# Attention and SoLU MoE on one core: the first two heads' products with v change from float32 to float16 parts, and the planner gets another transfer model

## The chip, the cores and the metric

The kernel runs on one core of a Trainium2 chip. Its time is the device time in microseconds (us) of that core, from launch to end; below it "span" is the part of it from the first to the last instruction of the profile. Engines are named as in the profile: PE is TensorE's matmul side and PEld its weight load, DVE VectorE, ACT ScalarE, POOL GpSimd, SP SyncE, which issues all DMA transfers here.

## The reference

Attention over 4 batches of 8 heads, 1152 keys of 64 dimensions, with queries averaged in pairs to 576 rows, and then a gated block over the 2304 resulting tokens of 512:

```python
q_pool = q.reshape(B, H, S // factor, factor, D).mean(axis=3)
scores = scale * np.matmul(q_pool, k.transpose(0, 1, 3, 2))
attn = softmax(scores)                       # max, exp, sum
x = np.matmul(attn, v)                       # (4, 8, 576, 64) -> (2304, 512)
...
h = x @ w_in
e = np.exp(h - h_max)
solu = h * e / (np.sum(e) + 1e-09)
ln = (solu - mu) / np.sqrt(var + 1e-06) * g_ln
return ln @ w_out
```

## The kernel before

**Tiles and stages.** The 32 heads are numbered 0 to 31, in 16 pairs P that share their loads. A head has 9 slots: in a slot, 128 keys against all 576 queries. A slot's scores are four float32 matmuls of 288 columns (`product`, rows `bank<-q,w`: high and low parts of q and k, in two halves f). ScalarE takes their exponentials, and TensorE multiplies these with v (`values`), adding over the 9 slots of a head in one PSUM bank. The products are made accurate by parts: in slots that are not "whole", ScalarE computes each exponential twice, once into a float16 tile `eh` and once into a float32 tile `e` (called e32 in the code), GpSimd subtracts (`rest`, row `eh<-e,eh`) so that the second half of the tile `eh` holds the float16 remainder, and `values` runs 15 float16 matmuls (`bank<-vhi,eh` and `bank<-vlo,eh`) for a slot in heads 0 to 7, 14 later. v itself is split per pair into `vhi` and `vlo` with a scale (`v_sum`, `v_turn`, `v_mul`, `v_hi`, `v_lo`). In "whole" slots, those below `KP["F"]`, here 18 and so heads 0 and 1, one exponential goes into a float32 tile `eh` and `values` runs 5 float32 matmuls with v as it is loaded (`vx`); the trace shows each as two instructions. These two heads need no `rest` and no split of v.

**Before a head's scores** come its maxima: 12 or 15 float32 matmuls of 384 columns (`bank<-w,q`), each followed by a DVE maximum (`mx<-bank`). Before these come, for each pair: loads of q, k and v; TensorE transposes; high and low parts of k and q by ACT and DVE; and copies from one half of the partitions to the other, by DMA (`k_put`: `w<-khi`, `w<-klo`; `k_again`: `w<-w`; `q_beside`: `q<-q`; the rows of maxima, `put`: `q<-c`).

**Weights** w_in and w_out come in 16 parts of 512 KB (`weight_part`, rows `raw<-in_moe_w_in_dram` and `..._w_out_dram`), each unpacked by two ACT passes (`up`, `un`), one POOL pass (`up<-up,un`), DVE and ACT passes, during heads 0 to 7. The gated block on finished tokens (`tokens`) is interleaved from head 8 on, and its last part runs alone behind head 31.

**What sets the order.** `Plan` collects all operations with a due time `at` in slots, simulates the five engines with a length for each operation, and writes the instructions out in the order of the simulated starts. An engine then executes its queue strictly in this order. A transfer's end in the simulation is: issue time plus a start delay, behind the transfers before it, plus its length `DMA(n)`, plus a delay for landing. The numbers of `KP` are due times and paces: `W` and `step` of the weight parts, `M` of the gated block, `P` of a pair's loads and splits, `N` of the maxima's lead, `CD` which slots take the float16 exponential by a DVE cast (`eh<-e`, L995) instead of a second ACT pass, `VM` who scales v, `F` the number of whole slots. TensorE gets filler transposes of the identity (`bank<-ident`) while it would wait at the start.

Of the kernel before, what the change touches and what calls it, by code (L numbers as in the profile page):

```python
# [17 lines left out]
ALU = mybir.AluOpType  # L18
AXX = mybir.AxisListType.X

KP = {'W': [2, 4, 5], 'step': 0.5, 'M': [77, 15.3, 7.49], 'TX': 113, 'TP': 72, 'win': 5.01, 'P': [22.92, 18.98, 13.92, 23.51, 26.08, 30.44], 'N': [13, 7], 'AV': 3.97, 'CD': [73, 13], 'VM': 'BCCCCABCBABBCCAC', 'AH': 8, 'OF': [5.14, 2.07, 10.29, 1.04, 2.66], 'N1': 10.46, 'warm': 1, 'ws': 1.3, 'GR': 1, 'GG': 12, 'b_eh': 6, 'b_w1': 4, 'V0': -53.76, 'VF': 1, 'QD': [0, 1], 'L0': 0.97, 'F': 18}
FIRST = KP.get("L0", 0.3)


# [15 lines left out]
class Plan:  # L40
# [61 lines left out]
    def run(self):  # L102
# [82 lines left out]
        while events:  # L185
# [67 lines left out]
                kind = o.kind  # L253
                length *= 1 if t > self.COLD else 2
            if e == "SP":
                busy[e] = t + 670 * o.calls
                dma = max(dma, t + 1100) + length
                o.end = dma + 1000
            else:
                busy[e] = o.end = t + length  # L260
            if o.mark is not None:
# [32 lines left out]
    return 1.885 * n + 148  # L294


def DMA(n, fast=1):
    return n / (360 if fast else 180)


@with_exitstack
def attention_solu_moe(
# [157 lines left out]
    def weight_part(n, at, src, i, f, dst_h, dst_l, dst):  # L460
# [15 lines left out]
            else:  # L476
                nc.sync.dma_start(out=raw, in_=src[rows, c])

        add("SP", DMA(4096 * 128), at - 3, fetch, [], [("raw", n)])
        if wide:  # L480


# [59 lines left out]
    def pair(P, at_k, at_q, at_v, loads):  # L542
# [23 lines left out]
        def load_v32(i):  # L566
            nc.sync.dma_start(out=v32(P)[:, i, :, 0:D], in_=v[b, h0 + i].rearrange("(p j) d -> p j d", j=NJ))
# [7 lines left out]
        kb = 128 * NJ * D * 4  # L575
        KT = ("vx", 0, "kt") if P == FN == 1 else ("kt", P)
        if P:
            add("SP", DMA(2 * kb, 0), at_lk, load_k, [("vx", 0, 0, "one")] if P == FN == 1 else [], [KT], calls=2)
        else:
            add("SP", DMA(kb), at_lk, lambda: load_k0(0), [], [("kt", 0, 0)])  # L580
        add("SP", DMA(2 * kb), at_lq, load_q, [], [("qt", P, i) for i in range(3)])
        if not P:
            add("SP", DMA(kb), at_lk + 0.1, lambda: load_k0(1), [], [("kt", 0, 1)])
        if P < FN:
            for i in range(2):
                add("SP", DMA(kb, 0), at_lv + i / 10, lambda i=i: load_v32(i), [], [("vx", 0, P % 2, "v", i)])
# [149 lines left out]
        def prep_q2(at):  # L736
            for i in range(2):
                ps, a = ("qps", (P, i)), at + 2 * i
                add("PE", TR(3 - i), a, lambda i=i: q_tr2(i), [("qt", P, 0)], [ps], also=[("q1", P), ("q2", P)], kind="whole")
                for odd in range(2):  # L740
                    n, o = ((384, 384), (256, 128))[i][odd], a + odd / 10
                    hi, lo = ("q1", P, i, odd), ("q2", P, 2 * i + odd)
                    add("ACT", ACT(n), o, lambda i=i, odd=odd: q_hi2(i, odd), [ps], [hi])
                    add("DVE", DVE(n), o, lambda i=i, odd=odd: q_lo2(i, odd), [ps, hi], [lo])
            for odd in range(2):
                add("SP", DMA(64 * 4 * 576, 0), at + 3, lambda odd=odd: q_beside(odd),
                    [("q1", P, i, odd) for i in range(2)], [("q1", P, 2, odd)], calls=2)
# [205 lines left out]
    def scores(g, at):  # L953
# [452 lines left out]
```

## Time and profile before

| | us |
|---|---|
| median of 3 runs | 729.42 (728.45 to 732.87) |
| the profiled execution | 732.07 |
| its span | 730.3 |
| PE busy | 686.0 (94%) |
| ACT busy | 534.7 (73%) |
| DVE busy | 506.5 (69%) |
| POOL busy | 486.4 (67%) |

Shares over the whole span mix stages. The stages here are the start (up to the first scores at 23.66 us), heads 0 and 1 (to 61.85), heads 2 to 7 (to 171.20), heads 8 to 30 (to 637.06), and head 31 with the rest of the gated block. Matmuls are pipelined, so a row's mean length is longer than the step from one matmul to the next; for matmuls the step is what loads TensorE.

### The profile page before, as it was taken

The page shows a single profiled execution, that of the slowest core. Times are in us where ns is not written, and L with a number is a line of the kernel's source. Part 1 is how long each engine was busy: PE and PEld are TensorE (multiplying, and loading weights), DVE is VectorE, ACT ScalarE, POOL GpSimd, SP SyncE. Part 2 cuts the span into 40 slices and gives each one's busy share as a digit, 9 for nine tenths or more (in the row PEclk, how much of TensorE's full clock was granted, in tenths as well). Part 3 has the DMA queues.
Part 4 walks back from the last instruction along what each step waited for, and adds up shares of the span by engine and source line. Part 5 has one row for each costly group of instructions (what it writes and reads, how often), then busy time and mean ns, then how long its engine had stood idle before and what let it go on. Part 6 is the DMA issues. An engine that isn't in the chain of part 4 may idle for free.

```text
span 730.3 us, 18791 instructions
## 1 busy us (share of the span) xinstructions
PE 686.0 (94%) x7048; PEld 598.7 (82%) x7048; DVE 506.5 (69%) x1221; ACT 534.7 (73%) x1327; POOL 486.4 (67%) x635
## 2 busy tenths in 40 slices
PE   7999787999989999999998999899999999999996
PEld 7989676777877888887887898788888898887885
DVE  5896786787887677877858684858586867425542
ACT  2656797989797687888778796778788877773432
POOL 1233796989788678697868677686967777681111
PEclk8999898999999999999999999999999999999999
DMA  8585566674453352536253434425445310000011
GB/s 206 156 210 152 152 161 160 180 182 101 123 120 96 90 135 53 133 88 163 41 128 98 113 84 113 101 65 135 101 102 130 91 42 18 17 16 22 15 30 29
DMA packets 78086, 75.79 MB, mean 104 GB/s; under 512 B 61108, under 2 KB 61228, under 8 KB 77996
## 3 DMA queue, kind: packets, MB, share of 16 engines
q1 hardware_dynamic: 77996, 74.60, 42.0%
q8 instruction: 55, 0.90, 0.5%
q14 instruction: 35, 0.29, 0.1%
HBM read 37.22 MB, written 4.72 MB: 57 GB/s over the span
## 4 chain that ended last, share of the span: by engine, by line
PE 66%; DVE 12%; ACT 8%; issue 5%; POOL 5%; DMA 3%; SPq 1%; ACTq 0%; DVEq 0%; POOLq 0%
PE bank L419 60%; DVE mx L859 4%; POOL eh L1005 3%; PE bank L1224 2%; ACT e L982 2%; PE bank L624 1%; ACT eh L988 1%; DVE q L422 1%; DVE eh L995 1%; DMA raw<-in_moe_w_in_dram 1%; PE bank L1374 1%; ACT e L988 1%; ACT q L718 1%; ACT eh L982 1%; DMA q<-q 1%
## 5 line engine op out<-in xcount | busy, mean ns | idle before, releaser
L1005 POOL TENSOR_TENSOR eh<-e,eh 128x64 f16<-128x64 f32 (+1 forms) x486 | 381.2, 809 | 123.7 <-ACT e L982 29.1
L859 DVE TENSOR_REDUCE mx<-bank 128x1 f32<-128x384 f32 x420 | 220.5, 550 | 79.4 <-PE bank L419 76.5
L419 PE MATMUL bank<-q,w 128*128 128x288 f32 (+1 forms) x1152 | 242.6, 314 | 11.3 <-ACT e L982 7.9
L419 PEld LDWEIGHTS bank<-q,w 128*128 128x128 f32 (+1 forms) x1152 | 188.2, 192 | 37.1 <-ACT e L982 17.8
L982 ACT ACTIVATE eh<-bank 128x288 f16<-128x288 f32 x376 | 159.1, 425 | 59.4 <-PE bank L419 57.2
L982 ACT ACTIVATE e<-bank 128x288 f32<-128x288 f32 x432 | 180.8, 427 | 22.5 <-POOL eh L1005 10.8
L419 PE MATMUL bank<-w,q 128*128 128x384 f32 x390 | 133.9, 371 | 12.9 <-DVE q L422 5.4
L419 PEld LDWEIGHTS <-eh 128*128 128x128 f16 x3834 | 126.6, 99 | 18.4 <-issue 11.2
L419 PE MATMUL bank<-vhi,eh 128*128 128x65 f16 x2484 | 136.2, 196 | 1.8 <-POOL eh L1005 0.9
L419 PE MATMUL bank<-vlo,eh 128*128 128x64 f16 x1350 | 133.1, 194 | 0.0
L419 PEld LDWEIGHTS bank<-w,q 128*128 128x128 f32 x390 | 72.8, 194 | 26.8 <-DVE mx L859 7.8
L1207 POOL TENSOR_TENSOR st<-st 128x1 f32<-128x1 f32 x54 | 23.4, 432 | 57.0 <-ACT junk L1194 53.9
L988 ACT ACTIVATE eh<-bank 128x576 f16<-128x576 f32 (+1 forms) x72 | 47.6, 667 | 12.6 <-PE bank L419 12.0
L493 POOL TENSOR_TENSOR up<-up,un 128x512 f32<-128x512 f32 x16 | 20.9, 1309 | 32.2 <-ACT un L486 14.9
L1155 DVE TENSOR_REDUCE st<-bank 128x1 f32<-128x512 f32 x36 | 24.7, 686 | 24.4 <-PE bank L419 24.3
L422 DVE TENSOR_TENSOR q<-bank,q 64x384 fp32r<-64x384 f32 (+2 forms) x63 | 28.8, 458 | 16.4 <-ACT q L718 13.4
L419 PE MATMUL bank<-woh,lh 128*128 128x512 f32 x104 | 34.3, 416 | 3.2 <-DVE e L1174 3.1
L988 ACT ACTIVATE e<-bank 128x576 f32<-128x576 f32 x54 | 36.1, 672 | 0.2 <-POOL eh L1005 0.2
L419 PE MATMUL bank<-wih,xl 128*128 128x512 f32 x104 | 33.8, 409 | 0.0
L419 PE MATMUL bank<-wol,lh 128*128 128x512 f32 x104 | 32.9, 399 | 0.0
L419 PE MATMUL bank<-wih,xh 128*128 128x512 f32 x104 | 32.7, 403 | 0.0
L419 PE MATMUL bank<-wil,xh 128*128 128x512 f32 x104 | 32.7, 398 | 0.0
(134 smaller groups left out, 1064.9 us busy)
## 6 DMA issues: line engine op xcount, KB each, us to landing
qt<-in_q_dram SPq DMA_DIRECT2D x16, 576.0 KB
w<-w SPq DMA_DIRECT2D x32, 288.0 KB
kt<-in_k_dram SPq DMA_DIRECT2D x30, 288.0 KB
vt<-in_v_dram SPq DMA_DIRECT2D x15, 576.0 KB
w<-khi SPq DMA_DIRECT2D x30, 288.0 KB
w<-klo SPq DMA_DIRECT2D x30, 288.0 KB
out_dram<-o SPq DMA_DIRECT2D x36, 128.0 KB
raw<-in_moe_w_in_dram SPq DMA_DIRECT2D x8, 511.6 KB
```

The costliest lines, as they stand in the source:

```text
L419: nc.tensor.matmul(out=o, lhsT=a, rhs=b, start=first, stop=last, skip_group_check=True)
L422: nc.vector.tensor_tensor(out=o, in0=a, in1=b, op=ALU.subtract)
L493: nc.gpsimd.tensor_tensor(out=up, in0=up, in1=tl["un", n].bitcast(F32), op=ALU.subtract)
L624: nc.tensor.transpose(ps[:, c, :], tl["kt", P][:, 3 * i + c].rearrange("p h d -> p (h d)"), ident)
L718: nc.scalar.copy(out=tl["q1", P][r, :, t, :], in_=ps)
L859: nc.vector.tensor_reduce(out=tl["mx", g][:, m, c:c + 1], in_=tl["nps", (g, m, c)], op=ALU.max, axis=AXX)
L982: nc.scalar.activation(out=tl[name, (g, j)][:, f * HALF:(f + 1) * HALF], in_=tl[tn(j, f), (g, j, f)], func=ACTF.Exp, scale=ESC,)
L988: nc.scalar.activation(out=new((name, (g, j)), [128, SQ * 4 // mybir.dt.size(dtype)], dtype)[:, 0:SQ].rearrange("p (f i) -> p f i", f=2), ...
L1005: nc.gpsimd.tensor_tensor(out=e[:, o:o + c.stop - c.start], in0=e32[:, c], in1=e[:, c], op=ALU.subtract)
L1155: nc.vector.tensor_reduce(out=st(f), in_=tl[H_[f]], op=ALU.max, axis=AXX)
L1207: nc.gpsimd.tensor_tensor(out=st(o), in0=st(a), in1=nhalf if b is None else st(b), op=op)
L1224: nc.tensor.transpose(ps[:, c, :], tl[E][:, o:o + 128], ident)
```

## The change

`F` goes from 18 to 0, so no slot is whole: heads 0 and 1 get the two exponentials, the `rest` and the float16 matmuls of the others, and pair 0 gets its v split. The simulation's transfers get a longer issue, start and landing delay and other rates, each transfer its own. Due times and paces in `KP` change, and with all of this the order of the program.

```diff
-KP = {'W': [2, 4, 5], 'step': 0.5, 'M': [77, 15.3, 7.49], 'TX': 113, 'TP': 72, 'win': 5.01, ... 'N': [13, 7], ... 'CD': [73, 13], 'VM': 'BCCCCABCBABBCCAC', ... 'F': 18}
+KP = {'W': [2, 4.47, 5], 'step': 0.66, 'M': [78.27, 15.99, 7.61], 'TX': 112, 'TP': 71, 'win': 4.11, ... 'N': [10.43, 7], ... 'CD': [67, 10], 'VM': 'BCCCAABBBABBCBAA', ... 'F': 0, 'DL': 2000}
...
             if e == "SP":
-                busy[e] = t + 670 * o.calls
-                dma = max(dma, t + 1100) + length
-                o.end = dma + 1000
+                busy[e] = t + 640 * o.calls
+                dma = max(dma, t + 1200) + length
+                o.end = dma + KP.get("DL", 1000)
...
-def DMA(n, fast=1):
-    return n / (360 if fast else 180)
+def DMA(n, rate=300):
+    return n / rate
...
-        add("SP", DMA(4096 * 128), at - 3, fetch, [], [("raw", n)])
+        add("SP", DMA(4096 * 128, 250), at - 3, fetch, [], [("raw", n)])
...
-                add("SP", DMA(64 * 4 * 576, 0), at + 3, lambda odd=odd: q_beside(odd),
+                add("SP", DMA(64 * 4 * 576, 200), at + 3, lambda odd=odd: q_beside(odd),
...
         def add_v(after):
             if P < FN:
-                if P < 2:
-                    add("POOL", 160, -13, lambda: nc.gpsimd.memset(v32(P)[:, :, :, D:D + 1], 1.0),
-                        [], [("vx", 0, P % 2, "one")])
                 return
```

The memset of `vx` moves to the place of the loads and stands under `if P < FN`; with `F` 0 it is not issued any more. Over the whole program the instructions change as follows: 90 float32 matmuls with `vx` go (180 rows in the trace), 270 float16 ones come; on ACT 17 `e` and 2 fewer `eh` passes of 576 columns, 2 more `e` and 16 more `eh` passes of 288, and 7 passes more for the split of v less one cast; on POOL 18 `rest` passes of 576 columns come, one `vlo` and the memset go; on DVE the casts L995 fall from 28 to 22, the scalings of v from 8 to 4, and two `vlo` passes come.

**POOL, the first rows after the set-up memsets.** Before:

```order
L813 MEMSET vx 128x18
L593 TENSOR_TENSOR qt<-qt 128x3x64
L602 TENSOR_TENSOR qt<-qt 128x576
L493 TENSOR_TENSOR up<-up,un 128x512 x3
L808 TENSOR_TENSOR vlo<-vt,vhi_76 128x1152
```

In the change (`e_314`, `e_345` and the next are the float32 exponentials of slots 0, 1 and following):

```order
L597 TENSOR_TENSOR qt<-qt 128x3x64
L606 TENSOR_TENSOR qt<-qt 128x576
L1006 TENSOR_TENSOR eh<-e_314,eh 128x576
L812 TENSOR_TENSOR vlo<-vt,vhi_75 128x1152
L1006 TENSOR_TENSOR eh<-e_345,eh 128x576
L1006 TENSOR_TENSOR eh<-e_359,eh 128x576
L493 TENSOR_TENSOR up<-up,un 128x512
L1006 TENSOR_TENSOR eh<-e_396,eh 128x576
```

The memset of `vx` no longer stands ahead of the pooling of q, and the rest passes of heads 0 and 1 and pair 0's `vlo` are new; the first weight parts (`up<-up,un`) are spread between them.

**ACT, the rows from the first scores on** (slots 0 to 3 of head 0). Before:

```order
L988 ACTIVATE eh<-bank 128x576
L627 CAST khi<-bank 128x384
L988 ACTIVATE eh<-bank 128x576
L627 CAST khi<-bank 128x384
L486 ACTIVATE un<-raw,ebias 128x512
L762 ACTIVATE vlo,am<-vt 128x1152
L988 ACTIVATE eh<-bank 128x576 x2
```

In the change:

```order
L989 ACTIVATE eh<-bank 128x576
L989 ACTIVATE e_314<-bank 128x576
L794 ACTIVATE vt<-vt,vs 128x1152
L989 ACTIVATE eh<-bank 128x576
L803 CAST vhi_75<-vt 128x18x64
L989 ACTIVATE e_345<-bank 128x576
L486 ACTIVATE un<-raw,ebias 128x512
L989 ACTIVATE eh<-bank 128x576
L989 ACTIVATE e_359<-bank 128x576
```

Each slot has two exponentials instead of one, and the two passes that split pair 0's v stand between the first ones.

**SP, the transfers for pair 2 and the weights around them** (head 2 of before). Before:

```order
L963 DMA w_1_74<-w_393 64x1152
L639 DMA w_698<-khi 64x1152
L639 DMA w_698<-klo 64x1152
L639 DMA w_718<-khi 64x1152
L639 DMA w_718<-klo 64x1152
L473 DMA raw<-in_moe_w_in_dram 128x4093 x2
L728 DMA q_727<-q_727 64x5x64 x2
L728 DMA q_727<-q_727 64x4x64 x2
L732 DMA zq_77<-q_727 64x64 x2
L561 DMA qt<-in_q_dram 128x1152
```

In the change:

```order
L643 DMA w_881<-khi 64x1152
L643 DMA w_888<-khi 64x1152
L643 DMA w_881<-klo 64x1152
L643 DMA w_888<-klo 64x1152
L964 DMA w_1_74<-w_555 64x1152
L732 DMA q_873<-q_873 64x5x64 x2
L732 DMA q_873<-q_873 64x4x64 x2
L736 DMA zq_77<-q_873 64x64 x2
L473 DMA raw<-in_moe_w_in_dram 128x4093
L561 DMA qt<-in_q_dram 128x1152
L473 DMA raw<-in_moe_w_in_dram 128x4093
```

The pair's exchange of q halves (`q<-q`) moves from behind two 512 KB weight parts to ahead of them.

## Rows read from the trace of the kernel before

**Rows 1.** Busy time by stage: start, heads 0 and 1, heads 2, 3, 4, 5, 6, 7, heads 8 to 30, the rest. The columns are the stretch in us from the span's start, its length, then the busy us of each engine, the granted TensorE clock, the share of the DMA engines and their GB/s.

```profile
core 0: us, PE busy (x) PEld busy (x) DVE busy (x) ACT busy (x) POOL busy (x), PEclk, DMA share, GB/s
0.00:23.66 23.66, 18.89 (x123) 18.16 (x123) 14.15 (x31) 4.79 (x10) 3.66 (x17) 0.86 0.75 207
23.66:61.85 38.19, 37.73 (x281) 34.73 (x279) 34.71 (x73) 26.91 (x48) 10.01 (x7) 1.00 0.64 158
61.85:86.47 24.62, 19.53 (x173) 16.96 (x172) 15.96 (x33) 17.53 (x32) 14.09 (x10) 0.86 0.60 155
86.47:101.72 15.25, 15.15 (x231) 13.80 (x231) 12.06 (x27) 13.69 (x26) 14.94 (x12) 1.00 0.67 159
101.72:122.76 21.04, 15.16 (x194) 13.66 (x191) 14.80 (x33) 15.86 (x30) 14.09 (x12) 0.84 0.75 183
122.76:137.55 14.79, 13.96 (x165) 11.58 (x165) 11.56 (x26) 14.63 (x27) 14.79 (x12) 1.00 0.48 129
137.55:157.29 19.74, 17.48 (x225) 14.64 (x224) 17.16 (x36) 17.71 (x33) 17.68 (x14) 0.91 0.93 238
157.29:171.20 13.91, 13.17 (x169) 11.62 (x168) 11.33 (x26) 13.56 (x26) 13.55 (x12) 1.00 0.33 76
171.20:637.06 465.86, 449.34 (x4949) 392.78 (x4947) 335.20 (x845) 368.80 (x1009) 356.39 (x494) 0.99 0.41 97
637.06:730.30 93.24, 85.54 (x560) 70.71 (x560) 39.60 (x97) 41.22 (x94) 27.21 (x50) 0.99 0.10 22
```

**Rows 2.** Timeline of the start, POOL and then ACT and DVE: start us, us, engine, line, operation, tiles, count, and in brackets the idle time before it with what ended it.

```profile
7.53 0.13 POOL L813 MEMSET vx<- 128x18 f32 x1 [5.37 <-DMA vx<-in_v_dram]
7.60 0.59 POOL L593 TENSOR_TENSOR qt<-qt 128x192 f32<-128x192 f32 x1
...
4.79 1.28 ACT L597 ACT_TABLE_LOAD   x1 [4.79 <-DMA qt<-in_q_dram]
8.22 0.35 ACT L597 COPY qt<-qt 128x192 f32<-128x192 f32 x1 [2.15 <-POOL qt L593]
8.48 1.22 ACT L649 CAST w<-bank 64x384 fp32r<-64x384 f32 x3
...
4.74 0.63 DVE L593 TENSOR_TENSOR qt<-qt 128x192 f32<-128x192 f32 x2 [1.50 <-DMA qt<-in_q_dram]
13.19 7.06 DVE L918 TENSOR_REDUCE mx<-bank 128x1 f32<-128x384 f32 x15 [0.54 <-PE bank L419]
```

**Rows 3.** Timeline of single slots: five float32 products with v of one slot on PE (ten rows of the trace) at 25.67 us, two exponentials of ACT at 28.46, 30 float16 weight loads (two slots) at 100.80.

```profile
25.67 1.22 PE L419 MATMUL bank<-vx,eh 128*128 128x65 f32 x10
28.46 1.19 ACT L988 ACTIVATE eh<-bank 128x576 f32<-128x576 f32 x2
...
100.80 0.96 PEld L419 LDWEIGHTS <-eh 128*128 128x128 f16 x30
```

**Rows 4.** Groups by line and shape, whole span: line, engine, operation, tiles, shape, count, busy us and mean ns of one, then the idle time before them.

```profile
L1005 POOL TENSOR_TENSOR eh<-e,eh 128x576 f16<-128x576 f32 x54 | 68.7, 1289 | 18.6 <-ACT e L988 16.6 <-PE bank L419 1.8
L808 POOL TENSOR_TENSOR vlo<-vt,vhi 128x1152 f16<-128x1152 f32 x12 | 27.6, 2301 | 0.3 <-ACT vhi L799 0.2
L493 POOL TENSOR_TENSOR up<-up,un 128x512 f32<-128x512 f32 x16 | 20.9, 1309 | 32.2 <-ACT un L486 14.9 <-ACT up L486 12.2 <-DVE mx L859 5.2
L799 ACT CAST vhi<-vt 128x1152 f16<-128x1152 f32 x12 | 14.2, 1187 | 2.3 <-DVE vt L792 2.3
L486 ACT ACTIVATE up<-raw,ebias 128x512 int32<-128x512 int8 x16 | 12.6, 786 | 8.0 <-DMA raw<-in_moe_w_in_dram 8.0
L790 ACT ACTIVATE vt<-vt,vs 128x1152 f32<-128x1152 f32 x4 | 5.2, 1301 | 0.0
```

**Rows 5.** The chain of work that ended last, around the three longest waits for a transfer: start us, us, what.

```profile
63.98 1.39 SPq L639
65.43 1.40 SPq L639
66.87 7.26 DMA raw<-in_moe_w_in_dram
...
107.93 5.67 DMA q<-q
...
450.78 5.66 DMA out_dram<-o
```

**Rows 6.** Who waited for whom, 61.85 to 122.76 us: engine, line, waited for, us in total, times, longest. The last line is from the same view of 23.66 to 61.85 us.

```profile
PEld bank L419 <- DVE q L422: 5.4, 2, 4.2
ACT up L486 <- DMA raw<-in_moe_w_in_dram: 5.1, 1, 5.1
PE bank L419 <- DMA q<-q: 4.4, 1, 4.4
...
ACT up L486 <- DMA raw<-in_moe_w_in_dram: 2.9, 1, 2.9
```

**Rows 7.** Granted clock in stretches behind these waits, columns as in rows 1.

```profile
76.50:83.40 6.90, 6.59 (x47) 5.64 (x47) 6.28 (x13) 5.21 (x9) 6.53 (x5) 0.51 0.47 133
110.70:117.50 6.80, 3.81 (x43) 3.52 (x44) 2.64 (x5) 2.98 (x7) 2.12 (x2) 0.50 0.58 182
117.50:148.20 30.70, 28.21 (x367) 23.95 (x364) 25.30 (x59) 29.20 (x55) 28.99 (x22) 1.00 0.68 162
```

**Rows 8.** The longest DVE cast and the POOL pass beside it, from the timelines of both engines.

```profile
388.99 2.37 DVE L995 CAST eh<-e 128x576 f16<-128x576 f32 x1 [0.20 <-ACT e L982]
...
388.75 2.30 POOL L808 TENSOR_TENSOR vlo<-vt,vhi 128x1152 f16<-128x1152 f32 x1
```

**Rows 9.** All casts of that line: shortest, median and longest duration in ns, first and last start.

```profile
L995 DVE CAST eh<-e x28: 442/460/2371, 183.7 to 651.2; 128x576 f16<-128x576 f32 x28
```

More of the change, by code (lines that the diff above doesn't have):

```diff
@@ L19 @@
 AXX = mybir.AxisListType.X
-KP = {'W': [2, 4, 5], 'step': 0.5, 'M': [77, 15.3, 7.49], 'TX': 113, 'TP': 72, 'win': 5.01, 'P': [22.92, 18.98, 13.92, 23.51, 26.08, 30.44], 'N': [13, 7], 'AV': 3.97, 'CD': [73, 13], 'VM': 'BCCCCABCBABBCCAC', 'AH': 8, 'OF': [5.14, 2.07, 10.29, 1.04, 2.66], 'N1': 10.46, 'warm': 1, 'ws': 1.3, 'GR': 1, 'GG': 12, 'b_eh': 6, 'b_w1': 4, 'V0': -53.76, 'VF': 1, 'QD': [0, 1], 'L0': 0.97, 'F': 18}
+KP = {'W': [2, 4.47, 5], 'step': 0.66, 'M': [78.27, 15.99, 7.61], 'TX': 112, 'TP': 71, 'win': 4.11, 'P': [22.92, 18.81, 13.57, 24.85, 27.38, 30.44], 'N': [10.43, 7], 'AV': 3.97, 'CD': [67, 10], 'VM': 'BCCCAABBBABBCBAA', 'AH': 8, 'OF': [5.14, 2.61, 11.19, 1.04, 2.66], 'N1': 12.32, 'warm': 1, 'ws': 1.3, 'GR': 1, 'GG': 10, 'b_eh': 6, 'b_w1': 4, 'V0': -55.58, 'VF': 1, 'QD': [0, 1], 'L0': 0.97, 'F': 0, 'DL': 2000}
 FIRST = KP.get("L0", 0.3)
@@ L577, in pair @@
         if P:
-            add("SP", DMA(2 * kb, 0), at_lk, load_k, [("vx", 0, 0, "one")] if P == FN == 1 else [], [KT], calls=2)
+            add("SP", DMA(2 * kb, 200), at_lk, load_k, [("vx", 0, 0, "one")] if P == FN == 1 else [], [KT], calls=2)
         else:
             add("SP", DMA(kb), at_lk, lambda: load_k0(0), [], [("kt", 0, 0)])
-        add("SP", DMA(2 * kb), at_lq, load_q, [], [("qt", P, i) for i in range(3)])
+        add("SP", DMA(2 * kb, 260), at_lq, load_q, [], [("qt", P, i) for i in range(3)])
         if not P:
@@ L584, in pair @@
         if P < FN:
+            if P < 2:
+                add("POOL", 160, -40, lambda: nc.gpsimd.memset(v32(P)[:, :, :, D:D + 1], 1.0),
+                    [], [("vx", 0, P % 2, "one")])
             for i in range(2):
-                add("SP", DMA(kb, 0), at_lv + i / 10, lambda i=i: load_v32(i), [], [("vx", 0, P % 2, "v", i)])
+                add("SP", DMA(kb, 200), at_lv + i / 10, lambda i=i: load_v32(i), [("vx", 0, P % 2, "one")],
+                    [("vx", 0, P % 2, "v", i)])
         else:
@@ L668, in prep_k @@
                     for l in range(2):
-                        add("SP", DMA(64 * S * 4), at + 4 * h + 0.5, lambda h=h, l=l: k_put(h, l),
+                        add("SP", DMA(64 * S * 4, 200), at + 4 * h + 0.5, lambda h=h, l=l: k_put(h, l),
                             [("klo" if l else "khi", P)], [("w1", 2 * P + h, l)])
@@ L745, in prep_q2 @@
             for odd in range(2):
-                add("SP", DMA(64 * 4 * 576, 0), at + 3, lambda odd=odd: q_beside(odd),
+                add("SP", DMA(64 * 4 * 576, 200), at + 3, lambda odd=odd: q_beside(odd),
                     [("q1", P, i, odd) for i in range(2)], [("q1", P, 2, odd)], calls=2)
-            add("SP", DMA(128 * 256, 0), at + 3, q_half, [("q1", P, 1, 0)], [("zq", P)], calls=2)
+            add("SP", DMA(128 * 256, 200), at + 3, q_half, [("q1", P, 1, 0)], [("zq", P)], calls=2)
         for i in range(3):
@@ L963, in k_again @@
             nc.sync.dma_start(out=w2[g % 2][0:D, :].bitcast(F32), in_=tl["w1", g][0:D, :].bitcast(F32))
-        add("SP", DMA(64 * S * 4), at - OF[0], k_again, [("w1", g)], [("w2", g)])
+        add("SP", DMA(64 * S * 4, 200), at - OF[0], k_again, [("w1", g)], [("w2", g)])
         def product(j, f):
```

## The prediction

> **What bounds the kernel now.** I read the table by stages first, because the change touches heads 0 and 1 and the order around them, and a share of the whole span says nothing about these. [rows 1] show three regimes. In heads 0 and 1, PE is busy 37.73 of 38.19 us, DVE 34.71, ACT 26.91, POOL only 10.01: TensorE is the bound and POOL has 28 us free. In heads 3, 5 and 7 the stretch is as long as POOL's or ACT's work (14.79 against 14.79 POOL and 14.63 ACT in head 5; 13.91 against 13.55 and 13.56 in head 7): there these two engines are the bound, with PE near them by its pipelined count. Heads 2, 4 and 6 are longer, 24.62, 21.04 and 19.74 us, with no engine full in the first two: they wait. From head 8 on PE is busy 449.34 of 465.86 us and bounds.
>
> What heads 2 and 4 wait for I read from the chain of work [rows 5] and the waits [rows 6]. In head 2 the chain stands 7.26 us for a weight part, which SP had issued behind four copies of k; ACT stood 5.1 us before `up`, and behind `up` in its queue stood the exponentials, so PE stood too. In head 4 it stands 5.67 us for the exchange of q halves, and PE waits 4.4 us for it. Behind both, TensorE's clock was granted at half, 0.51 for 6.90 us and 0.50 for 6.80 us [rows 7]: 1.2 GHz instead of 2.4.
>
> **The change, part by part.**
>
> *The start.* The memset of `vx` waited 5.37 us for the load of v and held the pooling of q's last third to 7.60 us, though q was there at 4.74, when DVE pooled its thirds [rows 2]. ACT's copy of that third waited 2.15 us for it after the table load (4.79 + 1.28 = 6.07 us), and the casts of k stood behind the copy, at 8.48. Without the memset ACT goes on at 6.07. The first maximum on DVE, at 13.19, moves ahead by up to 8.22 - 6.07 = 2.15 us by this chain, and by somewhat more since the new order transposes q ahead of k. On the other side all three low parts of q now stand ahead of the 15 maxima, which costs nothing at the end since one stood behind them. I take -2.9 us, with bounds of 0 (another transfer holds the start) and -4.
>
> *Heads 0 and 1, PE.* A slot's float32 products take 1.22 us; two slots of float16 loads take 0.96, so one takes 0.48 [rows 3]. 18 slots by 0.74 us are 13.3 us less on PE: 37.7 becomes about 24.4.
>
> *Heads 0 and 1, the others.* ACT gets 18 more exponentials: two take 1.19 us and the steps are under their length, so about 0.53 each, 9.5 us [rows 3]. Pair 0's scaling and cast of v add 1.30 + 1.19 us [rows 4], at most. In the new order two weight parts fewer are unpacked in these heads, about 3.7 us of ACT (two passes of 0.79, one cast, each counted by its step). 26.9 + 9.5 + 2.3 - 3.7 = 35.0 us. POOL gets 18 rests by 1.27 and one `vlo` of 2.30, less two passes of 1.3 [rows 4]: 10.0 + 22.9 + 2.3 - 2.6 = 32.6 us. DVE loses two parts' share, near 3.8 us: about 31. So ACT takes TensorE's place as the bound, at 35.0 us against 38.19. How tight it packs I take from heads 3, 5, 6 and 7, where ACT was busy 59.59 of 63.69 us, 0.936 [rows 1]: 35.0 / 0.936 = 37.4 us, -0.8. The 13.3 us of TensorE are thus nearly all not to be had. Bounds: 0.99, head 5's packing, gives 35.4 (-2.8); 0.81, between heads 6 and 4, gives 43 (+5).
>
> *Heads 2 to 7.* The float16 work is the same there. What changes is where the transfers stand. The new model lets a transfer land later in the simulation, so the planner leaves more slots between issue and use. In the order, the exchange of q for a pair stood a median of 1 slot ahead of its first reader, and now stands 3; the w_in parts stood 2 and now 3.1. The exchange of pair 2 is no longer behind two 512 KB parts. So I let the two chain waits go, 7.26 + 5.67 = 12.9 us. Two things come back: one w_in part, in head 3, still stands a quarter of a slot ahead of its `un` pass, and I price it by the shorter wait for a part, 2.9 us [rows 6]; and the two weight parts moved out of heads 0 and 1 lengthen heads 3, 5 and 7, which are full, by about 2. -12.9 + 2.9 + 2 = -8.0 us. The clock behind the waits is not counted apart: POOL was full at 6.53 of 6.90 us while it was low in head 2 [rows 7]. Bounds: all waits go and these heads run at their ACT or POOL load, about 94 of 109.4 us (-15.5); the waits only move to other places (+2).
>
> *From head 8.* PE's work is equal within a microsecond by counts, with some 4 us of the gated block moved into the last part. Six casts leave DVE and their second exponential goes to ACT, which has 97 us free of 465.86 [rows 1]. I take 0, bounded by the wait for a store of 5.66 us that a better model may remove [rows 5] and by the 4 us at the end: -6 to +4.
>
> The sum is -2.9 - 0.8 - 8.0 = -11.7 us. The profiled execution took 732.07 us, 2.65 over the median of the runs, so 720.4 for such an execution and 717.7 against the median 729.42. I predict **718 us**.
>
> *A rule against the change.* DVE and POOL block each other: the cast at 388.99 us took 2.37 us, until POOL's 2.30 us pass that began at 388.75 was done [rows 8], against a median of 460 ns for that cast [rows 9]. The Trainium skill, page "SBUF — State Buffer", section "SBUF: two separate sides", says why: the two share a pair of ports that one instruction holds whole, and the other fully blocks, if the DVE operation has two SBUF inputs or runs in a 2-port mode. By it, a now full POOL would hold the one such pass in heads 0 and 1 that matters, pair 1's scaling of v on DVE, for at most one rest, 1.29 us, and the sum would be 719.0 by it. The sum above leaves this out because DVE is 4 us below ACT there.
>
> **The rivals.**
>
> *The waits move (0.27).* The start gains 2.9, heads 0 and 1 gain 0.8, and heads 2 to 7 keep their length: a transfer is late at another place, for instance pair 1's copies of k, which the new order issues directly ahead of head 2's maxima in TensorE's queue. 729.42 - 3.7 = 725.7 us. For it speaks that the same sixteen weight parts and pair transfers go through the one SP queue, against it that the leads grew for most of them.
>
> *TensorE's clock falls in heads 0 and 1 (0.11).* TensorE is now free for a third of them: 24.4 us of work in 38. It was granted 1.00 in [rows 7]'s last row, with PE 28.21 of 30.70 busy, and 0.50 behind each long wait. If a wait of the size of head 4's 4.4 us falls early in heads 0 and 1 and the clock stays at half for them, 24.4 us become 48.8, which is 10.6 over the 38.2 of before; with the start gained and heads 2 to 7 unchanged, 729.42 - 2.9 + 10.6 = 737.1 us. It decides from the point at which the low clock lasts longer than PE's reserve covers: with 24.4 us of work in 37.4, at more than 13 us of low clock. Against it: the two low stretches seen last 7 us.
>
> *The front runs at its load (0.10).* All bounds on the good side: -4 - 2.8 - 13 = -19.8, 709.6 us.
>
> **How the numbers follow.** My forecast has 0.52, with its own range 711 to 723. A measurement of this kernel tells about 1% from no change, so faster means under 722.1, slower over 736.7. Nearly all of my forecast and the last rival are faster: 0.60. The moved waits and a little of the forecast are the same: 0.29. Slower has the clock's 0.11. The bounds, taken as independent, give about 10 us to either side, 708 to 728; with the last rival's neighbourhood and the moved waits' own spread the range is 706 to 731, and the clock's case stays out.
>
> **What would show it.** Right: the first scores at about 21 us instead of 23.66; ACT at 90% or more of heads 0 and 1, which last 36 to 39 us, with POOL over 30 us busy; no entry over 4 us for a weight part or for `q<-q` in the chain between 60 and 120 us, and no half clock there; head 8 starting near 160 us instead of 171.2. Wrong: heads 0 and 1 longer than 41 us (ACT packs worse, or TensorE's clock fell), or a new transfer wait in the chain before 165 us, or a stage from head 8 on that differs from 559 us by more than 6.

## The result and the profile after

The changed kernel takes 708.12 us (median of 4 runs, 706.60 to 709.15) against 729.97 for the kernel before in the same rounds (728.45 to 732.87): a ratio of 0.9694, with an interval of 0.9657 to 0.9731. The forecast was 718, the range 706 to 731. So the time lies inside the range, near its lower end, and the gain is 21.9 us where 11.7 were summed.

Busy time by stage of the kernel after, columns as in [rows 1], the stages cut at the same heads:

```profile
core 0: us, PE busy (x) PEld busy (x) DVE busy (x) ACT busy (x) POOL busy (x), PEclk, DMA share, GB/s
0.00:19.87 19.87, 18.26 (x135) 17.69 (x135) 14.69 (x31) 6.04 (x12) 3.75 (x16) 1.00 0.51 161
19.87:57.96 38.09, 32.98 (x384) 26.94 (x383) 31.91 (x70) 35.10 (x65) 31.45 (x24) 1.00 0.79 193
57.96:74.81 16.85, 15.25 (x192) 12.23 (x192) 16.01 (x35) 16.75 (x32) 14.93 (x13) 1.00 0.81 204
74.81:93.29 18.48, 16.56 (x200) 14.15 (x199) 14.55 (x30) 15.88 (x29) 16.47 (x13) 0.91 0.63 156
...
123.53:141.38 17.85, 16.22 (x224) 13.26 (x224) 15.53 (x34) 17.71 (x33) 16.64 (x14) 1.00 0.96 252
141.38:159.08 17.70, 14.45 (x202) 12.62 (x199) 14.67 (x29) 15.64 (x30) 16.45 (x13) 1.00 0.61 144
159.08:608.27 449.19, 441.87 (x4899) 388.12 (x4899) 331.95 (x835) 371.62 (x1019) 352.05 (x491) 1.00 0.42 99
608.27:705.10 96.83, 90.06 (x584) 73.95 (x582) 43.66 (x102) 42.59 (x98) 27.26 (x51) 0.99 0.10 22
```

Set against [rows 1], by subtraction: the start is 3.8 us shorter, heads 0 and 1 are 0.1 shorter, heads 2 to 7 (57.96 to 159.08, 101.1 us) 8.2, heads 8 to 30 16.7, and the last part is 3.6 longer. That is 25.2 us of the two profiled spans, 730.3 and 705.1. The one profiled before lay 2.1 us over its median, the one after 0.8 under it, which leaves about 22.

The start, from the timelines of POOL, ACT and DVE (to be read beside [rows 2]):

```profile
4.63 0.76 POOL L597 TENSOR_TENSOR qt<-qt 128x192 f32<-128x192 f32 x1 [2.48 <-DMA qt<-in_q_dram]
...
4.62 1.28 ACT L601 ACT_TABLE_LOAD   x1 [4.62 <-DMA qt<-in_q_dram]
5.92 0.35 ACT L601 COPY qt<-qt 128x192 f32<-128x192 f32 x1
...
10.65 7.04 DVE L919 TENSOR_REDUCE mx<-bank 128x1 f32<-128x384 f32 x15
```

POOL now waits for q alone and starts at 4.63 instead of 7.60. ACT's copy follows the table load at once, at 5.92 instead of 8.22, and the first maximum stands at 10.65 instead of 13.19. The clock of the start is 1.00, where it was 0.86 on the mean.

Who waited for whom in heads 2 to 7 after the change (57.96 to 159.08 us), the longest totals; [rows 6] are its counterpart:

```profile
PEld bank L419 <- DVE mx L860: 8.3, 17, 1.7
PEld bank L419 <- ACT e L989: 6.1, 13, 1.9
DVE mx L860 <- PE bank L419: 4.3, 9, 1.5
POOL eh L1006 <- ACT e L989: 3.9, 7, 1.0
PE bank L419 <- DVE mx L860: 3.8, 4, 1.6
```

No transfer is in this list, and none is in the chain, whose shares the page gives as

```profile
PE 66%; DVE 12%; ACT 10%; POOL 6%; issue 5%; ACTq 0%; DVEq 0%; POOLq 0%
```

so the waits of [rows 5], the store's at 450.78 us too, are gone. Of half clock, heads 2 to 7 of before had 6.90 and 6.80 us [rows 7] and 3.40 more in head 6; one stretch is left, in head 3. In these windows, columns as in [rows 7], the first row is what the engines did ahead of it:

```profile
74.00:78.10 4.10, 2.86 (x29) 2.27 (x26) 3.65 (x7) 3.40 (x6) 4.10 (x4) 1.00 0.88 203
78.10:81.50 3.40, 3.40 (x38) 3.40 (x38) 2.27 (x7) 2.67 (x5) 3.33 (x3) 0.50 0.92 233
```

From head 8 on nothing in the page says where 16.7 us went: PE was "busy" for 449.34 of 465.86 us and is so for 441.87 of 449.19. A matmul in that count includes what it waits for in the pipeline, so I worked from the starts of the PE rows instead. For each kind of matmul there is a distance to the next start that is the median where nothing holds it (30 ns for a float16 product with v, 134.5 for scores, 178 for maxima, 233 for the gated block, 110 for transposes). Summed over the rows of heads 8 to 30 this is "work"; what a distance has over its step counts as a "pause" if it is more than 0.15 us:

```
heads 8 to 30, us      work    pauses (count)    the rest    length
before                 422.3   25.2 (55)         18.4        465.9
after                  418.0   14.5 (40)         16.7        449.2
```

So 4.3 us of TensorE's work moved into the last part, which grew by 3.6, and 10.7 us of pauses went. "The rest" fell by 1.7; it also holds what half clock costs here, and of that before has two stretches (236.90 to 240.40 and 458.80 to 462.30 us, granted 0.51) and the kernel after one (160.10 to 163.50). Ordered by what ended them, the pauses behind ACT's exponentials fell from 9.2 to 5.4 us and those behind DVE's weighting of the gated block (L1174) from 4.4 to 0.8. The longest of before were 1.95 us at 455.7, behind the wait for the store, and 1.86 at 390.0, behind the cast of [rows 8]; the longest after is 1.10.

### The profile page after: what moved, and what is told of

Its sections match the earlier page's. It is cut to its first block, busy times and chain, and to the rows that moved or that the text cites. A ratio compares the mean times of both kernels' runs of the same rounds, so it can differ in the third digit from the quotient of the medians.

```text
span 705.1 us, 19052 instructions
## 1 busy us (share of the span) xinstructions
PE 672.5 (95%) x7151; PEld 582.0 (83%) x7151; DVE 509.0 (72%) x1216; ACT 551.3 (78%) x1366; POOL 507.8 (72%) x651
## 4 chain that ended last, share of the span: by engine, by line
PE 66%; DVE 12%; ACT 10%; POOL 6%; issue 5%; ACTq 0%; DVEq 0%; POOLq 0%
PE bank L419 59%; POOL eh L1006 5%; DVE mx L860 4%; PE bank L1225 2%; ACT e L983 2%; DVE q L422 2%; PE bank L1375 2%; PE bank L628 1%; ACT eh L983 1%; ACT e L989 1%; ACT eh L989 1%; ACT q L722 1%; ACT e L1168 1%; PE bank L712 1%; DVE bank L497 1%
## 5 line engine op out<-in xcount | busy, mean ns | idle before, releaser
L1006 POOL TENSOR_TENSOR eh<-e,eh 128x64 f16<-128x64 f32 (+1 forms) x504 | 405.0, 828 | 109.7 <-ACT e L983 28.8
L419 PE MATMUL bank<-q,w 128*128 128x288 f32 (+1 forms) x1152 | 238.3, 312 | 6.7 <-ACT e L989 3.3
L419 PEld LDWEIGHTS bank<-q,w 128*128 128x128 f32 (+1 forms) x1152 | 184.6, 191 | 34.8 <-ACT e L983 12.1
L983 ACT ACTIVATE eh<-bank 128x288 f16<-128x288 f32 x392 | 167.0, 429 | 49.1 <-PE bank L419 46.1
L983 ACT ACTIVATE e<-bank 128x288 f32<-128x288 f32 x434 | 183.4, 433 | 16.7 <-POOL eh L1006 13.1
L419 PEld LDWEIGHTS <-eh 128*128 128x128 f16 x4104 | 134.0, 98 | 18.4 <-issue 8.3
L419 PE MATMUL bank<-vhi,eh 128*128 128x65 f16 x2664 | 144.2, 195 | 3.0 <-POOL eh L1006 2.9
L419 PE MATMUL bank<-vlo,eh 128*128 128x64 f16 x1440 | 140.4, 193 | 0.0
L989 ACT ACTIVATE eh<-bank 128x576 f16<-128x576 f32 x70 | 47.5, 680 | 3.5 <-PE bank L419 3.4
L989 ACT ACTIVATE e<-bank 128x576 f32<-128x576 f32 x71 | 48.4, 681 | 0.7 <-POOL eh L1006 0.4
L422 DVE TENSOR_TENSOR klo<-bank,khi 128x384 fp32r<-128x384 f32 x45 | 24.8, 552 | 19.1 <-ACT khi L631 18.9
L419 PE MATMUL bank<-woh,ll 128*128 128x512 f32 x104 | 32.1, 397 | 0.0
```

What stands on the lines that cost most here:

```text
L419: nc.tensor.matmul(out=o, lhsT=a, rhs=b, start=first, stop=last, skip_group_check=True)
L422: nc.vector.tensor_tensor(out=o, in0=a, in1=b, op=ALU.subtract)
L983: nc.scalar.activation(out=tl[name, (g, j)][:, f * HALF:(f + 1) * HALF], in_=tl[tn(j, f), (g, j, f)], func=ACTF.Exp, scale=ESC,)
L989: nc.scalar.activation(out=new((name, (g, j)), [128, SQ * 4 // mybir.dt.size(dtype)], dtype)[:, 0:SQ].rearrange("p (f i) -> p f i", f=2), ...
L1006: nc.gpsimd.tensor_tensor(out=e[:, o:o + c.stop - c.start], in0=e32[:, c], in1=e[:, c], op=ALU.subtract)
```

## The experiments

Three things change at once: `F` (float32 or float16 products in heads 0 and 1), the simulation's transfer model, and the due times in `KP`. My theory after the result: the new order as a whole has fewer waits, each part alone puts some of them elsewhere, and heads 8 to 30 are the due times' work. The rivals: one part alone (the float16 products, or the transfer model as the prediction had it) brings the gain; or the casts that left DVE do. Times are medians; the stages are those of one profiled execution each, in us. The kernel before took 726.52 to 734.96 us in 15 runs, and its median moved from 728.82 to 730.01 between the rounds, so a difference of one or two us between two rows says nothing.

| kernel | F | model | due times | start | heads 0-1 | heads 2-7 | heads 8-30 | last part | median, ratio to before (interval) |
|---|---|---|---|---|---|---|---|---|---|
| before | 18 | old | old | 23.7 | 38.2 | 109.4 | 465.9 | 93.2 | 729.97 |
| e1_f0 | 0 | old | old | 19.1 | 46.7 | 97.3 | 463.1 | 93.3 | 721.49, 0.9885 (0.9830 to 0.9941) |
| e2_model | 18 | new | old | 21.4 | 47.9 | 98.5 | 461.2 | 93.2 | 722.78, 0.9897 (0.9864 to 0.9930) |
| e3_kp | 18 | old | new | 22.6 | 41.0 | 99.0 | 450.2 | 98.6 | 712.32, 0.9767 (0.9707 to 0.9828) |
| e5_f0_model | 0 | new | old | 20.1 | 42.0 | 98.2 | 460.2 | 93.3 | 717.34, 0.9847 (0.9816 to 0.9878) |
| e4_f0_kp | 0 | old | new | 19.2 | 42.0 | 98.4 | 450.4 | 99.2 | 710.74, 0.9767 (0.9725 to 0.9808) |
| e6_model_kp | 18 | new | new | 20.2 | 54.5 | 100.9 | 447.7 | 96.8 | 721.73, 0.9912 (0.9877 to 0.9946) |
| after | 0 | new | new | 19.9 | 38.1 | 101.1 | 449.2 | 96.9 | 708.12, 0.9694 (0.9657 to 0.9731) |

### Each part alone

**F alone.**

```diff
-'F': 18}
+'F': 0}
```

> The kernel before with F = 0 alone; transfer model, due times and paces stay the old ones. Theory A (the change's gain is the start without the memset and the order that the new transfer model makes; float16 products give nothing, since ACT takes TensorE's place in heads 0 and 1): about 726 us, start 3.9 us earlier, heads 0 and 1 within 37 to 41 us, heads 2 to 7 near 109 us with a wait for a weight part still there, heads 8 to 30 near 466 us. Theory C (the 13 us less of TensorE work carry the gain): 717 us or less.

Measured: 721.49 us, between the two theories. Heads 2 to 7 lose 12.1 us with the old model and the old times, so the new model is not needed for that; an entry of 5.73 us for `q<-q` still stands in their chain. But heads 0 and 1 grow by 8.5. The chain between 25 and 66 us has the reason:

```profile
41.47 6.01 DMA raw<-in_moe_w_in_dram
```

A weight part is late there now. The clock was then granted at half, 0.50 from 45.60 to 55.80 us. The order around the wait is another, and the wait came with it: the rival "the waits move", for this kernel.

**The model alone.**

```diff
-                busy[e] = t + 670 * o.calls
-                dma = max(dma, t + 1100) + length
-                o.end = dma + 1000
+                busy[e] = t + 640 * o.calls
+                dma = max(dma, t + 1200) + length
+                o.end = dma + KP.get("DL", 1000)
```

with `'DL': 2000` and the rates of the change; `F` stays 18.

> The kernel before with the new transfer model alone (issue, start and landing delays, rates); F stays 18, due times and paces the old ones, memset where it was. Theory A: the waits for transfers in heads 2 to 7 go (8 us) and the pauses of TensorE in heads 8 to 30 shrink as in the change (13 us): about 710 us. Theory B (due times and paces make the gain from head 8 on): about 721 us, heads 8 to 30 still near 466 us.

Measured: 722.78 us. Heads 2 to 7 fall to 98.5 us, but both waits stand in heads 0 and 1 now; the chain of 25 to 60 us:

```profile
30.40 8.53 DMA raw<-in_moe_w_in_dram
...
43.70 0.52 SPq L728
44.26 4.98 DMA q<-q
```

These are waits of the two kinds of [rows 5] again, with about the same lengths (7.26 and 5.67 there), 36 and 64 us earlier. A model that lets transfers land later did not remove such waits; with the old due times they stand in another place.

**The due times alone.** The `KP` line of the change, with `'F': 18` and without `DL`.

> The kernel before with the new due times and paces alone (F stays 18, old transfer model). Theory A: 728 us, plus or minus 4, with transfer waits over 4 us in heads 2 to 7. Theory B: heads 8 to 30 fall to about 450 us and the whole to about 716 us.

Measured: 712.32 us, 17.7 us under before, and the only one of the three that takes more than 5 us off heads 8 to 30 (450.2), with the longer last part. Heads 2 to 7 fall to 99.0 as well, though their chain has three transfers of over 4 us:

```profile
74.52 5.73 DMA qt<-in_q_dram
...
106.09 4.01 DMA raw<-in_moe_w_out_dram
...
127.77 6.07 DMA w<-klo
```

### Two parts together

**F and the times, old model.** The kernel after with the old delays and rates.

> The change with the old transfer model (old issue, start and landing delays and rates; F = 0 and the new due times and paces stay). The times and paces alone gave heads 8 to 30 in 450.2 us, the model alone 461.2. Theory B (due times and paces carry the gain from head 8 on, the model little): heads 8 to 30 within 447 to 453 us and the whole within 4 us of the change, 706 to 712. Theory A (the order that the model makes carries it): heads 8 to 30 near 460 us, the whole 718 or more.

**F and the model, old times.** The kernel after with the old `KP` line but `'F': 0, 'DL': 2000`.

> F = 0 and the new transfer model with the old due times and paces: the last corner of the three parts. Heads 2 to 31 took 668 us before, 653 to 654 with F = 0 or the model alone, 645 to 648 in all four kernels with the new times. Theory B (the new times are worth 6 to 8 us from head 2 on, whatever else): heads 2 to 31 in 651 to 655 us. Heads 0 and 1 in 38 us if no transfer is late there, 42 to 48 if a weight part is, as it was in both parts alone: the whole 712 to 722. Rival (F = 0 and the model together make the order of the change): within 4 us of the change, 706 to 712.

**The model and the times, float32 products.** The kernel after with `'F': 18`; the memset of `vx` is issued again, here ahead of the loads of v.

> The change with F = 18: heads 0 and 1 go by float32 products again, with the new model, times and paces. If the float16 products give nothing (ACT takes TensorE's place in heads 0 and 1): within 4 us of the change, 706 to 712, heads 0 and 1 in 37 to 41 us with TensorE full. If the 13 us less of TensorE work carry part of the gain: 716 us or more.

Measured: 710.74, 717.34 and 721.73 us. Two things follow from the table. Heads 8 to 30 are 447.7 to 450.4 us in all four kernels with the new times and 460.2 to 465.9 in all four with the old: there the due times decide. In the front no part has a price of its own. By the medians `F` is worth 8.5 us with both others old, 5.4 beside the new model, 1.6 beside the new times (the two ratios are equal, so this is nothing that can be told), and 13.6 beside both. The last comes from e6_model_kp, where heads 0 and 1 take 54.5 us. Its windows there, columns as before:

```profile
38.00:42.50 4.50, 2.26 (x21) 2.05 (x19) 3.06 (x9) 2.39 (x5) 1.44 (x2) 1.00 1.02 204
42.50:56.20 13.70, 13.42 (x57) 13.23 (x58) 3.93 (x9) 5.03 (x8) 4.79 (x3) 0.50 0.72 178
```

and its chain:

```profile
42.04 0.70 DVE q L901
42.78 14.02 PE bank L419 x59
```

TensorE had 2.52 us without work before 42.78, behind DVE's `q`. From 42.5 on the clock was granted at half for 13.7 us, though TensorE worked through all of them, and since with float32 products it is the bound of these heads, it had no reserve: 13.7 us at half cost about 6.9. Its busy time in heads 0 and 1 is 49.80 us against 37.73 in [rows 1]. The other 5 us are products: all 180 rows with `vx` stand ahead of head 2's first scores here, in before only 140, and the four slots between are 4.9 us by [rows 3]. At the end of the stretch TensorE runs only 17 rows from 67.20 to 73.30 us, while the chain goes through DVE with the last maxima of head 2. So by this estimate the half clock is about half of the 13.6 us; the split of the others is not shown. In e3_kp, with the same products, no clock falls in these heads and they take 41.0 us.

Heads 2 to 7 of e4_f0_kp are 2.7 us shorter than those of after, which have no transfer in their chain, and yet its chain has two there:

```profile
88.35 5.67 DMA raw<-in_moe_w_out_dram
129.69 4.13 DMA q<-q
```

So a wait on the chain is not a price to be added or taken off whole. The three of e3_kp say the same, and r3_who below, with 7.20 us for `w<-w` and 4.44 for `g_sb` behind it and heads 2 to 7 in 98.6. Such an entry runs from the transfer's issue to its landing, and not only while an engine stands: for `q<-c` e6_model_kp has an entry of 2.30 us at 73.11, and PE stood 0.36 us.

### The memset alone

```diff
+            if P < 2:
+                add("POOL", 160, -40, lambda: nc.gpsimd.memset(v32(P)[:, :, :, D:D + 1], 1.0),
+                    [], [("vx", 0, P % 2, "one")])
...
-                if P < 2:
-                    add("POOL", 160, -13, lambda: nc.gpsimd.memset(v32(P)[:, :, :, D:D + 1], 1.0),
-                        [], [("vx", 0, P % 2, "one")])
```

The kernel before, with the memset ahead of the loads of v, which now wait for it.

> The kernel before with the memset of vx issued ahead of the load of v and nothing else changed. Theory A: the start's gain alone: scores begin near 20 us instead of 23.66, the whole is 726 us (725 to 728). Rival: the start is held by another transfer, or what is gained is waited for later: 729 us.

Measured: 727.66 us, a ratio of 0.9972 (0.9942 to 1.0003, 10 runs). The start falls from 23.66 to 19.28 us. Heads 2 to 7 keep 108.1, and their chain keeps both waits of [rows 5] (with a third, 6.20 us for `q<-q`, at 136.99):

```profile
63.00 6.90 DMA raw<-in_moe_w_in_dram
...
103.39 4.37 DMA q<-q
```

The mechanism of the start is shown by its place in the profile, but of its 4.4 us only about 2 reach the end, and the interval touches no gain at all.

### Which due times

Each of these is the kernel after with one group of entries set back. `M` holds the start, spacing and rate of the gated block's parts, `OF` offsets within a head, `N`, `N1` and `P` leads of the preparations, `win` how far ahead of the due times the planner may go, `CD` and `VM` which engine converts what, `GG`, `TX` and `TP` how slots are grouped and where their scores stand in PSUM. The weight parts' `W` and `step` and the first pair's `V0` were not set back.

```diff
# r1_moe
-'M': [78.27, 15.99, 7.61], 'OF': [5.14, 2.61, 11.19, 1.04, 2.66]
+'M': [77, 15.3, 7.49], 'OF': [5.14, 2.07, 10.29, 1.04, 2.66]
# r5_m: 'M' alone
# r2_lead
+'N': [13, 7], 'N1': 10.46, 'win': 5.01, 'P': [22.92, 18.98, 13.92, 23.51, 26.08, 30.44]
# r3_who
+'CD': [73, 13], 'VM': 'BCCCCABCBABBCCAC', 'GG': 12, 'TX': 113, 'TP': 72
```

> The change with the old due times of the gated block (M and OF). Theory B1 (the block's wider spacing, 15.99 slots instead of 15.3, makes TensorE's pauses from head 8 on shrink and moves 4 us of its work to the end): heads 8 to 30 go back to about 462 us, the last part to 93, the whole to about 718. Rival B2 (the maxima's lead does it): heads 8 to 30 within 3 us of 449, the whole 705 to 711.

> The change with the old start, spacing and length of the gated block's tiles (M) but the new due times inside a tile (OF). With M and OF old, heads 8 to 31 took 555 us against 546, and heads 2 to 7 95 against 101. If the spacing M moves these: heads 8 to 31 in 553 to 557 us, the last part near 93. If the due times inside a tile do: 545 to 549 us, the last part near 97. The whole 705 to 713 in both.

> The change with the old lead of the maxima and of a pair's preparation (N, N1, P and win). Theory B1 (the gated block's spacing): heads 8 to 30 within 3 us of 449, the whole 705 to 712. Rival B2 (a shorter lead of the maxima, 10.43 slots instead of 13, takes them out of the way of the scores): heads 8 to 30 back to about 462 us, the whole about 720.

> The change with the old choice of who casts and scales (CD, VM, GG, TX, TP): 28 DVE casts instead of 22. If the casts that POOL holds up cause TensorE's pauses from head 8 on (the pauses ended by DVE's weighting pass were 4.4 us before and 0.8 in the change): these pauses come back and heads 8 to 31 take 3 to 6 us more, 711 to 714 us. Rival (the block's spacing M and OF does it): within 2 us of the change.

| kernel | heads 0-1 | heads 2-7 | heads 8-30 | last part | work, pauses in 8-30 | median, ratio to before (interval) |
|---|---|---|---|---|---|---|
| after | 38.1 | 101.1 | 449.2 | 96.9 | 418.0, 14.5 | 708.12, 0.9694 (0.9657 to 0.9731) |
| r1_moe | 38.1 | 94.6 | 461.9 | 93.4 | 424.0, 22.9 | 711.21, 0.9771 (0.9735 to 0.9807) |
| r5_m | 39.5 | 99.7 | 459.6 | 92.7 | 423.0, 21.0 | 712.99, 0.9793 (0.9758 to 0.9828) |
| r2_lead | 41.0 | 101.3 | 452.6 | 96.2 | 418.4, 19.5 | 713.12, 0.9797 (0.9754 to 0.9840) |
| r3_who | 38.1 | 98.6 | 452.3 | 98.3 | 418.6, 18.4 | 709.13, 0.9735 (0.9707 to 0.9763) |

`M` alone brings heads 8 to 30 back to the old times' length and the last part too. The stages of r5_m from head 8 on, to be set beside those of after:

```profile
158.83:618.38 459.55, 447.31 (x4925) 392.45 (x4925) 335.85 (x847) 374.31 (x1028) 353.12 (x492) 1.00 0.41 97
618.38:711.03 92.65, 85.40 (x557) 69.65 (x555) 40.02 (x90) 39.81 (x91) 27.40 (x50) 1.00 0.10 22
```

After head 30 PE has 557 rows here, 560 in before and 584 in after: the gated block's last products are done earlier, and in exchange heads 8 to 30 hold 5 us more work and 6.5 us more pauses. On the whole `M` is worth 4.9 us here, and 3.1 together with `OF`, far from the 718 that the block's theory gave r1_moe, though its heads 8 to 30 came out as it said. Heads 2 to 7 of r1_moe give 6.5 us back: they run there at ACT's load, with no half clock,

```profile
57.89:152.51 94.62, 87.32 (x1127) 72.71 (x1126) 81.42 (x177) 93.42 (x170) 90.10 (x70) 1.00 0.75 190
```

and why the block's due times do this to heads ahead of the block is open. The leads are worth 5.0 and act in several stages. What r3_who sets back is worth about 1 us, within what can be told apart. But from head 8 on it costs 4.5 us, as its first theory said, against 6.2 for `M`, 9.2 for `M` with `OF` and 2.7 for the leads; before is 13.1 longer there than after. The pauses behind DVE's weighting stayed at 1.0 us in r3_who, so the six casts that left DVE are not why those went; the pauses behind ACT's exponentials rose to about 10 us, from 5.4.

### Is ACT the bound of heads 0 and 1

The kernel after, without the second exponential and the rest pass in slots 0 to 17. The products that took the rest read the high part there, so PE's work is the same, and the low part of the weights is missing from the output of these heads.

```diff
+                        c += 0 if NJ * g + j < 18 else LO
-                        mm(o, e[:, LO + c:LO + c + 128], vh, False, last)
+                        mm(o, e[:, c:c + 128], vh, False, last)
...
+            bare = NJ * g + j < 18
-            exps = (("eh", F32),) if exact else (("eh", F16), ("e32", F32))[by_dve:]
+            exps = (("eh", F32),) if exact else (("eh", F16),) if bare else (("eh", F16), ("e32", F32))[by_dve:]
...
-            if not exact:
+            if not exact and not bare:
```

> The change without the float32 exponentials and the rest passes of slots 0 to 17: the third group of products takes the high part again, so the products of heads 0 and 1 lack their remainder. It leaves out 18 ACT passes of 0.53 us (9.5 us) and 18 POOL passes of 1.27 us; TensorE's instructions stay. If ACT and POOL bound heads 0 and 1 of the change (35.1 and 31.5 us busy of 38.1): these heads fall to 32 to 35 us, where DVE with 31.9 us is next. If waits for transfers or DVE hold them: 37 us or more.

Measured: 712.62 us (0.9776, 0.9748 to 0.9803), and heads 0 and 1 take 46.0 us instead of 38.1, with about 9.5 us of ACT and 23 of POOL less asked of them. The windows say why this answers nothing on the bound:

```profile
38.00:42.50 4.50, 2.42 (x14) 1.79 (x14) 4.30 (x13) 1.12 (x3) 0.43 (x1) 1.00 1.10 248
...
42.50:49.30 6.80, 5.94 (x35) 5.95 (x36) 2.75 (x6) 3.77 (x7) 3.66 (x2) 0.50 0.96 210
```

The order is a new one. At 38 to 42.5 us, the turn from head 0 to head 1, DVE is busy for 4.30 of 4.50 us and PE for 2.42, waiting for it in part, and the clock stands at half behind it, here for 6.80 us and again from 63.0. Against that, e4_f0_kp has one weight part more in its heads 0 and 1:

```profile
19.19:61.18 41.99, 33.12 (x414) 27.67 (x413) 35.12 (x76) 39.19 (x71) 34.62 (x26) 1.00 0.78 196
```

ACT has 4.1 us more there than in after, and the stretch is 3.9 longer; ACT's share is 0.933, the prediction's packing was 0.936. But DVE and POOL rise by 3.2 each, and the chain has a wait of 3.27 us for `q<-q` in this stretch. That ACT bounds is consistent with this, and not shown.

## Why the prediction was right in its range, and where its sum was not

*The start* (forecast -2.9, measured -3.8 in the profile): right in its steps, since the pooling, the copy and the first maximum came at the times that the chain gave. The first maximum is 2.5 us earlier. The other 1.2 us, which the sum did not have, lie behind the last maximum: TensorE gets from its filler transposes to the next one (L894, after the change L895) 1.4 us after DVE's `g_sb` starts in before (20.63 to 21.99 us) and 0.4 us after it now (17.80 to 18.20). The half clock of before's start is gone too, and what it cost there is not separated. The memset's kernel shows that part of such a start is given back later.

*Heads 0 and 1* (forecast -0.8, measured -0.1). ACT was forecast at 35.0 us and has 35.10, POOL at 32.6 and has 31.45, DVE at 31 and has 31.91. Of PE's 13.3 us saved nothing was to be had, as the prediction said. But 13.3 was not the saving in this stretch: ahead of head 2's first scores stand the products of 14 slots in before (140 rows with `vx`) and of 16 in after, and by the steps PE's work there went from 34.6 to 26.7 us. The busy 32.98 holds waiting on top of that. The step's packing of 0.936 came out as 0.921.

*Heads 2 to 7* (forecast -8.0, measured -8.2). That the size came out is in good part luck. The prediction gave it to the new transfer model and to two waits that go. The runs show that any of the three parts takes these heads to 97.3 to 99.0 us, with waits for transfers still in their chain in e1_f0 and e3_kp, and that with `F` alone or the model alone a wait of the same kind stands in heads 0 and 1. The clock, which the sum did not count, stood at half for 17.1 us in these heads of before and for 3.4 after; its share of the 8.2 us is not separated. Heads 0 to 7 together are 147.5 us in before, 144.0 and 146.4 with these two, 139 to 141 with the due times alone, with `F` and either other part, and with all three, and 155.4 in e6_model_kp. The price of the waits, 12.9 us taken off whole, is not confirmed either: e4_f0_kp has 5.67 and 4.13 us of waits on its chain there and is shorter than after.

*From head 8* (forecast 0, bounds -6 to +4; measured -16.7 + 3.6 = -13.1): **this is the step that failed.** It lies outside its own bounds, and the sign of being wrong that was named for it came (546.0 us from head 8 on instead of 559, more than 6 off). That the whole lies inside the range all the same is luck: the range reached so far down for gains in the front, not for one of this size from head 8 on. The step counted the work, found it equal within a microsecond, and priced only the longest wait (5.66 us for a store) as what might go. The work is equal indeed; what moved is 4 us of it into the last part, which cost 3.6 there as the bound allowed. But the pauses between PE's rows are 55 of under 2 us, 25.2 us in total, and none of the views that I read has them in one row: PE's busy share of 0.96 hides them, and the chain calls most of them by the engine that came last. I took a change of due times in a stage where PE is "full" as free. The runs put it on the due times (all four kernels with them); of the 16.7 us in heads 8 to 30 `M` alone brings 10.4 back, and with the last part 6.2 of 13.1. How `M` takes the pauses away is open: in r5_m they are behind DVE's maxima (7.7 us, against 4.2 in after) rather than where before had them, so it isn't one wait that comes back.

*The other signs.* The start, heads 0 and 1, the chain and the start of head 8 came as the prediction's list had them; "no half clock" between 60 and 120 us did not (78.10 to 81.50).

*The rivals.* "The waits move" (0.27) did not happen in the whole change and did in its parts, 3 to 4 us under the time given for it: 721.5 and 722.8 against 725.7. The rival of the clock (0.11) did not happen in the change either: the granted clock is 1.00 through heads 0 and 1. But its mechanism is real, and stronger than [rows 7] let me think: in e6_model_kp a stretch of 13.7 us at half follows a gap of 2.5 us. There it meets float32 products. With float16 ones, as the rival had it, 10.2 us at half stand in heads 0 and 1 of e1_f0, which take 46.7 us, with a late transfer ahead of them. The rival's limit was worked out wrongly: x us at half cost x/2 of work, so a reserve of 13 us lasts for 26 us of low clock and not for 13, if the work can be spread so. "The front runs at its load" (0.10) named about the right time, 709.6, for a wrong reason: heads 0 to 7 did not run at their load.

*The rule on the ports.* By the Trainium skill, page "SBUF — State Buffer", section "SBUF: two separate sides", whichever of a POOL instruction and a DVE one in a 2-port mode starts first holds the shared ports to its end. If the scaling runs in such a mode, this trace agrees, with the cost on the other side than the prediction had it: DVE's scaling of v started first, at 39.03 us, and took 0.88 us (0.82 before), and the two rests from 39.25 on took longer than a later two.

```profile
39.25 3.04 POOL L1006 TENSOR_TENSOR eh<-e,eh 128x576 f16<-128x576 f32 x2
...
45.36 2.53 POOL L1006 TENSOR_TENSOR eh<-e,eh 128x576 f16<-128x576 f32 x2 [0.82 <-ACT e L989]
```

POOL lost 0.5 us, and was busy for 31.45 of 38.09 us. The casts of [rows 9] are now

```profile
L996 DVE CAST eh<-e x22: 441/627/2086, 154.8 to 612.8; 128x576 f16<-128x576 f32 x22
```

six fewer with a longer median, 627 ns against 460, so a cast did not get shorter.

## What to carry to other kernels

In a stage whose bound engine is "busy" for 96%, sum its short pauses from the starts of its rows before pricing a new order there at nothing; here 55 of them, none over 2 us, held 25 us and 11 of it went. In a program with one fixed order, a wait that one edit removes can stand again a few heads earlier, so judge a stretch by its sum (heads 0 to 7 together), not by the waits in its chain. And an edit has no price apart from the order that it stands in: the same float16 products were worth 1.6 us, which is no more than noise, in one order and 13.6 in another. Whether they serve there as a reserve for stretches at half clock is not shown.

## What the runs showed of the hardware that was not expected

The granted clock stayed at half for 13.7 us while TensorE had work without a break: 13.42 us busy of 13.70 in e6_model_kp, on scores, maxima and float32 products of 65 columns. It was also at half for 13.7 us in heads 0 and 1 of e2_model, with TensorE busy for 6.13 of them, and for 10.2 us in e1_f0. In [rows 7] it was low for 6.9 us at most. Ahead of those of e6_model_kp and e9_bare TensorE had been busy for 2.26 and 2.42 of 4.50 us; the one of after, behind 2.86 of 4.10, lasted 3.4. What decides how long it lasts was not tried.

The chain's waits for a transfer come back with lengths of the same order wherever they stand: 6.01, 6.90, 7.26 and 8.53 us for a part of w_in on the chains of e1_f0, e7_memset, before and e2_model, and from 3.27 us (e4_f0_kp) to 6.28 (e7_memset) for the exchange of q halves, with 5.67 in before.
